# A planner for side work replaced by a fixed table of slots, in an attention block fused with a gated feed-forward

## The chip, the cores and the metric

The kernel runs on one core of one Trainium2 chip. The metric is device microseconds of one execution. A core has five engines with instruction streams of their own, which run in order and wait for each other through semaphores: TensorE (PE, matmuls; PEld is its weight load), VectorE (DVE), ScalarE (ACT), GpSimd (POOL) and SyncE (SP, which here issues DMAs). Lines such as L800 are lines of the kernel before.

## The reference

```python
def _attn_ref(x, inducing):                  # x: 4 x 12416 x 128, inducing: 32 x 128
    ...
    def mab(q, kv):
        s = scale * (q @ kv.transpose(0, 2, 1))
        s = s - s.max(-1, keepdims=True)
        a = np.exp(s)
        a /= a.sum(-1, keepdims=True) + 1e-09
        return a @ kv
    h = mab(I, x)                            # stage 1: 32 queries over 12416 tokens
    return mab(x, h)                         # stage 2: 12416 queries over 32 keys

def _moe_ref(x, w_gate, w_val, w_out):       # 128 -> 1536 -> 128, on all 49664 tokens
    gate = 1.0 / (1.0 + np.exp(-(x @ w_gate)))
    val = x @ w_val
    return gate * val @ w_out
```

The output of the attention block is the input of the feed-forward.

## The kernel before

A batch has 12416 tokens, 97 chunks of 128: six groups of 16 chunks and a group of one chunk (s = 6). Since the second attention has only 32 keys, h is folded into the weights: `hw` holds h times the gate and value weights, and the gate and value of a token are a product of its 32 normalised weights (a2) with `hw`, on 32 rows of TensorE.

**The main loop** (the last lines before the launch) runs over 776 steps, which alternate between a wide one (two of the twelve 128-wide blocks of the hidden layer, tile 128 x 1024) and a narrow one (one block, 128 x 512), for four chunks at a time. A wide and a narrow step are a *slot*: 388 slots, 96 per batch and four at the end for the four one-chunk groups together. In step t, `product(t)` fills v on TensorE (`hidden_mm`, L773), fills the gate of step t + 2, and has VectorE form u = (tanh + 1) * v (L800); `gate(t + 2)` is ScalarE's tanh (L791); `project` adds u times the output weights into `acc` on TensorE (L830), 12 matmuls a slot, and every fourth slot ends in ScalarE's eviction of `acc` (L849) and a store through SP. Gate and value each have one PSUM bank pair and one bank, `acc` has a bank, and one bank, tag `m`, serves all side work.

**A wide product's wait.** It needs tanh(t) and v(t). Where `lag` (what the planner believed ScalarE to be late by) is under LATE, the wait for the tanh is replaced by a wait for the last matmul of the gate fill of t + 2, which itself waits for that tanh.

**Side work** prepares the next batch and the next groups while the loop runs:
- stage 1 of the next batch, per group: `s1_score` (scores in `m` on TensorE, maximum nm on VectorE, L204), `s1_exp` (a1T on ScalarE, L217), `s1_turn_dma` (a1: a transpose by DMA, issued from SP, L241; the one-chunk group is turned on TensorE), `s1_sum` (32 matmuls hp, L253, and the copy hst on ScalarE, L265);
- `combine`: the minimum of minima ml (VectorE, then `join_min` on GpSimd), weights w1 (ScalarE, L355), join hx and its tree (GpSimd, L358 and L297), l_ps and h_ps (L378, L383), li and hT on VectorE, two halves of `hw` (`hw_fill`, copy L394);
- stage 2, per group: `s2_score` (two halves of eight matmuls, L403), `s2_take` (sc on ScalarE, L442), `s2_lower_pool` (maximum tree on GpSimd, L452 to L457), `s2_exp_low` (e on ScalarE, L466), `s2_sum_pool` (L474), `s2_inverse_pool` (L498 ff.) and `s2_spread` (a2n, L520) on GpSimd, `s2_turn_dma` (a2r: a transpose by DMA from SP, L531). The last group of a batch carries the one-chunk group along (17 columns);
- loads: `x_load` (from GpSimd's queue, L92) and `x_transpose_dma` (xT, from SP's queue, L101).

**What sets their order.** Each piece is a Python generator. `beside(slot)`, called after the wide step, and `beside_late()`, called after the narrow one, advance all active generators, stage 2 first, then combine, then stage 1. A generator that says "take" waits for the bank `m`; one that says a number waits until its cost fits a running estimate, `behind`, of how late ScalarE is (it falls by ROOM = 0.33 a slot and rises by EVICT = 0.48 per eviction; large operations go into the late call). Thus the slots in which side work lands differ from group to group. Every engine gets its instructions in the order in which this program issues them.

Of the kernel before, what the change touches and what calls it, by code (L numbers as in the profile page):

```python
# [13 lines left out]
ALU = mybir.AluOpType  # L14
# [8 lines left out]
S1_LAG = 6  # L23
S1_FIRST = 7
S2_LEAD = 28
S2_LAG = 8
COMBINE_LAG = 6
SUM_LAG = 9
ROOM = 0.33
MOST = 0.67  # L30
EVICT = 0.48
SMALL = 0.2
LATE = 0.55
# [3 lines left out]
def kernel(  # L37
# [136 lines left out]
    behind = [0.0]  # L174
# [92 lines left out]
    def stage1(b, s):  # L267
        yield "take"
        s1 = s1_score(b, s, "m")
        behind[0] = max(behind[0] - 0.6, -0.2)  # L270
        yield
        yield 0.48
        a1T = s1_exp(b, s, s1)
        yield "give"
        yield
        if groups[s][1] == GC:
            a1 = s1_turn_dma(b, s, a1T)
            for _ in range(S1_LAG):
                yield
            yield "take"  # L280
        else:
            yield "take"
            a1 = s1_turn_copy(s, s1_turn_pe(b, s, a1T))
            yield
        yield 0.18
        s1_sum(b, s, a1, "m")
        yield "give"
# [55 lines left out]
    def combine(b):  # L343
        q = b % 2
        nm1, hst = nm1s[q], hsts[q]
        while summed[b] < NS:
            yield
        ml = bp.tile([P, 1], F32, tag="ml")
        nc.vector.tensor_reduce(out=ml[:], in_=nm1[:], axis=AX.X, op=ALU.min)
        col = join_min(bp, ml)  # L350
        for _ in range(COMBINE_LAG):
            yield
        yield 0.2
        w1 = bp.tile([P, NS], F32, tag="w1")
        nc.scalar.activation(out=w1[:], in_=nm1[:], func=AF.Exp, bias=col[:], scale=-1.0)  # L355
        yield
        hx = bp.tile([P, NS, C + 1], F32, tag="hx", bufs=1)
        nc.gpsimd.tensor_tensor(  # L358
            out=hx[:],
            in0=hst[:],  # L360
            in1=w1[:].unsqueeze(2).to_broadcast((P, NS, C + 1)),
            op=ALU.mult,
        )
        add_tree(hx, NS)
        e32l = bp.tile([P, m], F32, tag="e32l")
        nc.gpsimd.tensor_scalar(
            out=e32l[:],
            in0=e32[:],
            scalar1=hx[:, 0, C : C + 1],
            scalar2=TINY,  # L370
            op0=ALU.mult,
            op1=ALU.add,
        )
        for _ in range(SUM_LAG):
            yield
        yield "take"
        l_ps = ps.tile([P, m], F32, tag="m", name="l_ps")
        nc.tensor.matmul(l_ps[:], ones[:], e32l[:], start=True, stop=True)  # L378
        li = l_inverse(l_ps[:])
        yield "give"  # L380
        yield "take"
        h_ps = ps.tile([P, m], F32, tag="m", name="h_ps")
        nc.tensor.matmul(h_ps[:], hx[:, 0, 0:C], e32[:], start=True, stop=True)  # L383
        h_take(b, h_ps[:], li)
        yield "give"
        yield


        hwt = bp.tile([P, NI, P], F16, tag="hw", bufs=B)
        for hf in range(2):  # L390
            yield "take"
            hw_ps = hw_fill(b, hf, "m")
            yield 0.37
            nc.scalar.copy(out=hwt[:, ts(hf, NI // 2), :], in_=hw_ps[:])  # L394
            yield "give"
        hw[b] = hwt
# [41 lines left out]

    taking = [0]
# [99 lines left out]
    def stage2(b, c, soon=False, far=0):  # L539
        while b not in hT16 or taking[0]:  # L540
            yield
        taking[0] += not soon
        n = GC + far
        if not soon:
            sc = s2p.tile([P, GC + NLO, m], F32, tag="sc", name="sc", bufs=1)
        if far:
            yield "take"
            s2 = ps.tile([P, GC, m], F32, tag="m", name="s2_ps")
            s2_score(b, 0, 0, far, s2, True)
            yield  # L550
            yield 0.08
            s2_take(sc, GC, far, s2)
            yield "give"
        yield "take"
        s2 = ps.tile([P, GC, m], F32, tag="m", name="s2_ps")
        s2_score(b, c, 0, GC // 2, s2)
        yield
        s2_score(b, c, GC // 2, GC, s2, not soon)
        if soon:
            hi, lo = s2_max(GC, s2)  # L560
            yield
            yield
            yield 0.48
            e = s2_exp(GC, s2, hi, lo)
            yield "give"
        else:
            yield
            yield 0.48
            s2_take(sc, 0, GC, s2)
            s2_lower_pool(n, sc)  # L570
            yield "give"
            for _ in range(S2_LAG):
                yield
            yield 0.48
            e = s2_exp_low(n, sc)
            taking[0] = 0
            yield
        sme = s2_sum_pool(n, e)
        yield
        yield  # L580
        rs = (s2_inverse if soon else s2_inverse_pool)(n, sme)
        a2n = s2_spread(n, e[:, 0:n, :], rs, nc.gpsimd)
        for _ in range(2 if soon else 4 if far else 5):
            yield
        s2_turn_dma(b, c, GC, a2n, "a2r")
        if far:
            s2_turn_dma(b, 0, far, a2n, "a2l", GC)
# [205 lines left out]
    def product(t):  # L793
# [21 lines left out]
    lag = []  # L815
# [4 lines left out]
    def project(upto, now, room):  # L820
        while queue and queue[-1][0] < upto and room > 0:
# [23 lines left out]
            elif j == NJ - 1:  # L845
                behind[0] += EVICT
                block = blocks[st["block"]]
                o32 = op.tile([P, BC, C], F32, tag="o32")
                nc.scalar.mul(out=o32[:], in_=acc[0][0][:], mul=0.5)  # L849
# [6 lines left out]
    work = []  # L856
    loads = []
    base = [first_step[(b, 0)] // 2 for b in range(B)]
    SG = first_step[(0, 1)] // 2
    for b in range(B):  # L860
        at = base[b]
        for s in range(1, NG):
            c = groups[s][0]
            soon = b == 0 and s == 1
            far = NLO if s == NG - 1 else 0
            work.append(
                (
                    max(0, at + SG * s - S2_LEAD),
                    0,
                    lambda b=b, c=c, soon=soon, far=far: stage2(b, c, soon, far),  # L870
                )
            )
        if b + 1 < B:
            for g in range(NS):
                loads.append((at + (5 if b == 0 else 3) * g, "t", b + 1, g))
                if b == 0 and 3 <= g < NG:
                    loads.append((at + (3, 14, 17)[g - 3], "x", 1, g))
                work.append((at + S1_FIRST + 6 * g, 2, lambda b=b, g=g: stage1(b + 1, g)))
            work.append((at + S1_FIRST + 6 * NS, 1, lambda b=b: combine(b + 1)))
            work.append((at + SG * NG - S2_LEAD, 0, lambda b=b: stage2(b + 1, NLO)))  # L880
        if b + 2 < B:
            for g in range(NG):
                loads.append((at + 24 + 9 * g, "x", b + 2, g))
    loads.sort(key=lambda e: e[0])
    work.sort(key=lambda e: e[0])

    active = []
    holder = [None]
    free_at = [0]
    slot_now = [0]  # L890

    def taken():
        return holder[0] is not None or slot_now[0] < free_at[0]

    def fits(cost):
        slot = slot_now[0] % 4
        at = behind[0] + cost
        if cost <= SMALL and slot == 2 and any(g["cost"] > SMALL for g in active):
            return False
        return at <= MOST and at + (EVICT if slot == 0 else EVICT - ROOM if slot == 3 else 0.0) <= MOST  # L900

    def advance(gen, late=False):

        if gen["cost"]:
            if late == (gen["cost"] <= SMALL) or not fits(gen["cost"]):
                return
            behind[0] += gen["cost"]
            gen["cost"] = 0.0
        elif late:
            return  # L910
        if gen["ask"]:
            if taken():
                return
            holder[0] = gen
            gen["ask"] = False
        while True:
            try:
                said = next(gen["it"])
            except StopIteration:
                active.remove(gen)  # L920
                return
            if isinstance(said, float):
# [86 lines left out]
```

## Time and profile before

| | |
|---|---|
| median of 3 runs | 731.3 us (730.89 to 731.36) |
| the profiled execution | 730.88 us, span 729.1 us |
| granted TensorE clock, mean | 0.991 |
| busy, share of the span | DVE 97%, ACT 93%, PE 89%, POOL 57% |
| first product starts, last one ends | 33.3 us, 725.2 us |
| chain that ended last | DVE 53%, issue 23%, PE 14%, ACT 5%, DMA 2% |
| wide product, narrow product | 388 of 1212 ns, 387 of 676 ns |
| wide tanh, narrow tanh | 388 of 1034 ns, 388 of 609 ns |
| a1 transposes, issue to landing | 2.4 / 2.6 / 7.2 us (least, median, most) |
| xT transposes, issue to landing | 2.2 / 4.8 / 11.4 us |

How to read it: durations are those of single instructions in one profiled execution, and neighbours on one engine overlap a little, so sums of durations come out above busy times. A group's line ends with the engine's idle time just before its instructions and what ended it. A wait is put down to the semaphore that came last. In the page, queue q1 carries what SP issues and q0 what GpSimd issues.

### The profile page before, as it was taken

The page shows a single profiled execution, that of the slowest core. Times are in us where ns is not written, and L with a number is a line of the kernel's source. Part 1 is how long each engine was busy: PE and PEld are TensorE (multiplying, and loading weights), DVE is VectorE, ACT ScalarE, POOL GpSimd, SP SyncE. Part 2 cuts the span into 40 slices and gives each one's busy share as a digit, 9 for nine tenths or more (in the row PEclk, how much of TensorE's full clock was granted, in tenths as well). Part 3 has the DMA queues.
Part 4 walks back from the last instruction along what each step waited for, and adds up shares of the span by engine and source line. Part 5 has one row for each costly group of instructions (what it writes and reads, how often), then busy time and mean ns, then how long its engine had stood idle before and what let it go on. Part 6 is the DMA issues. An engine that isn't in the chain of part 4 may idle for free.

```text
span 729.1 us, 21430 instructions
## 1 busy us (share of the span) xinstructions
PE 647.7 (89%) x8406; PEld 393.3 (54%) x8406; DVE 708.5 (97%) x873; ACT 675.6 (93%) x1011; POOL 419.1 (57%) x702
## 2 busy tenths in 40 slices
PE   6798998999998989989988899899999899898887
PEld 4355555555554555555555555555555555555555
DVE  4799999999999999999999999999999999999998
ACT  4689999999999999999999999999999999999996
POOL 3554655886764548488567265388486575555200
PEclk9799999999999999999999999999999999999999
DMA  9899736243259272436148541320222122121211
GB/s 174 142 163 197 154 74 138 60 83 81 75 109 181 51 137 75 95 74 118 45 97 159 110 76 45 74 74 31 75 60 69 49 60 60 51 67 45 60 45 45
DMA packets 117750, 65.19 MB, mean 89 GB/s; under 512 B 101361, under 2 KB 102033, under 8 KB 117649
## 3 DMA queue, kind: packets, MB, share of 16 engines
q1 hardware_dynamic: 111936, 49.81, 29.3%
q0 software_dynamic: 5440, 13.90, 11.2%
q8 instruction: 65, 1.06, 0.6%
q14 instruction: 37, 0.29, 0.1%
q10 hardware_dynamic: 272, 0.13, 0.1%
HBM read 27.80 MB, written 25.43 MB: 73 GB/s over the span
## 4 chain that ended last, share of the span: by engine, by line
DVE 53%; issue 23%; PE 14%; ACT 5%; DMA 2%; POOL 1%; DVEq 1%; ACTq 0%; POOLq 0%
DVE u L800 51%; PE acc_ps L830 6%; PE v_ps L773 5%; ACT t L791 5%; DMA xn<-in_x_dram 2%; DVE nm L204 1%; DVEq L800 1%; PE hp_ps L253 1%; PE g_ps L773 1%; POOL xn L92 0%; PE s_ps L192 0%; ACT a1T L217 0%; POOL sum L474 0%; DVE li L302 0%; PE s_ps L427 0%
## 5 line engine op out<-in xcount | busy, mean ns | idle before, releaser
L800 DVE SCALAR_TENSOR_TENSOR u<-t,v_ps 128x1024 f16<-128x1024 f16 (+1 forms) x777 | 678.1, 943 | 3.0 <-PE g_ps L773 1.3
L791 ACT ACTIVATE t<-g_ps 128x1024 f16<-128x1024 f32 (+1 forms) x776 | 595.1, 822 | 32.8 <-ACT t L791 20.0
L773 PE MATMUL v_ps<-a2r,hwt 32*128 32x512 f16 (+1 forms) x1188 | 293.5, 371 | 65.0 <-DVE u L800 61.8
L830 PE MATMUL acc_ps<-wo,u 128*128 128x128 f16 x4656 | 328.3, 220 | 0.3
L830 PEld LDWEIGHTS <-u 128*128 128x128 f16 x4656 | 262.5, 98 | 89.8 <-issue 88.6
L773 PE MATMUL g_ps<-a2r,hwt 32*128 32x512 f16 (+1 forms) x1188 | 296.6, 377 | 0.0
L773 PEld LDWEIGHTS <-hwt 32*128 32x128 f16 x2400 | 93.3, 91 | 200.6 <-issue 154.8
L474 POOL TENSOR_TENSOR sum<-e 128x256 f32<-128x256 f16 (+1 forms) x23 | 15.4, 670 | 156.1 <-ACT e L466 152.1
L520 POOL TENSOR_TENSOR a2n<-e,rs 128x2048 f16<-128x2048 f16 (+2 forms) x24 | 86.2, 3593 | 6.8 <-PE g_ps L773 2.8
L498 POOL TENSOR_TENSOR near<-sme,minus 128x16 f32<-128x16 f32 (+1 forms) x22 | 65.2, 2965 | 1.7
L849 ACT ACTIVATE o<-acc_ps 128x512 f32<-128x512 f32 x96 | 58.4, 608 | 0.5 <-PE acc_ps L830 0.5
L453 POOL TENSOR_SCALAR rise<-rise 128x256 f32<-128x256 f32 (+6 forms) x110 | 51.0, 463 | 9.7
L452 POOL TENSOR_TENSOR rise<-sc 128x256 f32<-128x256 f32 (+1 forms) x22 | 16.3, 740 | 30.8 <-ACT sc L442 30.8
L454 POOL TENSOR_TENSOR top<-top,rise 128x128 f32<-128x128 f32 (+3 forms) x88 | 28.3, 321 | 7.3
L474 POOL TENSOR_TENSOR sum<-sum 128x128 f32<-128x128 f32 (+3 forms) x92 | 28.3, 308 | 7.2
L452 POOL TENSOR_TENSOR rise<-top 128x128 f32<-128x128 f32 (+3 forms) x88 | 27.2, 309 | 6.9
L457 POOL TENSOR_TENSOR sc<-sc,top 128x512 f32<-128x512 f32 (+1 forms) x22 | 23.9, 1084 | 1.7
L403 PEld LDWEIGHTS <-xT 128*128 128x128 f16 x388 | 13.4, 97 | 12.2 <-issue 12.2
L403 PE MATMUL s_ps<-hT,xT 128*128 128x32 f16 x388 | 18.2, 179 | 0.3 <-DVE hT L307 0.3
L454 POOL TENSOR_TENSOR top<-sc,rise 128x256 f32<-128x256 f32 (+1 forms) x22 | 16.3, 739 | 1.8
L217 ACT ACTIVATE a1T<-s_ps,nm 128x512 f16<-128x512 f32 (+1 forms) x24 | 15.1, 630 | 1.7 <-DVE nm L204 1.7
L204 DVE TENSOR_REDUCE nm<-s_ps 128x1 f32<-128x512 f32 (+1 forms) x24 | 14.7, 614 | 0.9 <-PE s_ps L192 0.9
(116 smaller groups left out, 229.9 us busy)
## 6 DMA issues: line engine op xcount, KB each, us to landing
out_dram<-o SPq DMA_DIRECT2D x96, 256.0 KB, 2.3
xn<-in_x_dram POOLq DMA_DIRECT2D x19, 512.0 KB, 6.8
xn<-in_x_dram POOLq DMA_DIRECT2D x4, 544.0 KB, 5.9
a2r<-a2n SPq DMA_TRANSPOSE x29, 4.6
xn<-in_x_dram POOLq DMA_DIRECT2D x1, 384.0 KB, 15.3
wg<-in_moe_w_gate_dram POOLq DMA_DIRECT2D x1, 384.0 KB, 4.6
wv<-in_moe_w_val_dram POOLq DMA_DIRECT2D x1, 384.0 KB, 6.4
wo<-in_moe_w_out_dram POOLq DMA_DIRECT2D x1, 384.0 KB, 5.2
```

The costliest lines, as they stand in the source:

```text
L403: nc.tensor.matmul(s2[:, j, :], xT[b][:, c + j, :], hT16[b][:], start=(j == 0), stop=whole and j == j1 - 1, skip_group_check=True,)
L452: nc.gpsimd.tensor_tensor(out=r, in0=far, in1=near, op=ALU.subtract)
L453: nc.gpsimd.tensor_scalar_max(out=r, in0=r, scalar1=0.0)
L454: nc.gpsimd.tensor_tensor(out=top[:, 0:n, 0:w], in0=near, in1=r, op=ALU.add)
L474: nc.gpsimd.tensor_tensor(out=d[:, 0:n, :], in0=src[:, :, 0:w], in1=src[:, :, w : 2 * w], op=ALU.add)
L498: nc.gpsimd.tensor_tensor(out=near[:, 0:n], in0=sme[:, 0:n], in1=minus1[:, 0:n], op=ALU.pow)
L520: eng.tensor_tensor(out=a2n[:, 0:n, :, :], in0=e.unsqueeze(2).to_broadcast((P, n, 4, m)), in1=rs.unsqueeze(2).unsqueeze(3).to_broadcast((P ...
L773: st[what + "end"] = nc.tensor.matmul(pt[:, k, col : col + nb * P], hw[b][r : r + 32, j // 2, :], a2r[r : r + 32, o : o + nb, :].rearrange ...
L791: st["tanh"] = nc.scalar.activation(out=st["t"][:], in_=st["g"][:], func=AF.Tanh, scale=0.5)
L800: u = nc.vector.scalar_tensor_tensor(out=st["u"][:, :, c:e], in0=st["t"][:, :, c:e], scalar=1.0, in1=st["v"][:, :, c:e], op0=ALU.add, op1= ...
L830: nc.tensor.matmul(acc[0][(i // 2) % len(acc[0])][:, i, :], st["u"][:, k, ts(i, P)], wo16[:, j, :], start=(j == 0 and i in ((0, 2) if len( ...
L849: nc.scalar.mul(out=o32[:], in_=acc[0][0][:], mul=0.5)
```

## The change

The planner (generators, costs, `behind`, `lag`) is removed. A table `plan` maps a slot and a call (early or late) to a list of closures; `plan_stage1`, `plan_combine` and `plan_stage2` enter the steps of a piece at slots written out by hand, counted from the first slot o of a batch, in a pattern that repeats every 16 slots. The loop then calls what stands at each slot. The functions that issue the instructions stay the same, with these differences: every wide product from step 4 to the last but two waits for the gate fill of t + 2; l and h share one tile of bank `m` and are issued in the same slot; the join of the next h is entered four slots after `least`, two slots before the take and maximum tree of the batch's last group; the one-chunk group is scored before groups 4 and 5; some loads move to other slots.

The core of the diff, with the table in full:

```diff
+    plan = {}
+    def at(slot, make, late=False):
+        plan.setdefault((slot, late), []).append(make)
...
+    def plan_stage1(b, s, score, total):
+        st = {}
+        full = groups[s][1] == GC
+        def begin():
+            st["s1"] = s1_score(b, s, "m")
+        def weigh():
+            st["a1T"] = s1_exp(b, s, st["s1"])
...
+        at(score, begin)
+        at(score + 1, weigh, late=full)
+        at(score + 2, turn)
+        at(total, lambda: s1_sum(b, s, st["a1"], "m"))
...
+    def plan_combine(b, lead, weights, fill):
...
+        def total():
+            lh = ps.tile([P, 2, m], F32, tag="m", name="lh_ps")
+            nc.tensor.matmul(lh[:, 0, :], ones[:], st["e32l"][:], start=True, stop=True)
+            nc.tensor.matmul(lh[:, 1, :], st["hx"][:, 0, 0:C], e32[:], start=True, stop=True)
+            st["lh"], st["li"] = lh, l_inverse(lh[:, 0, :])
...
+        at(lead, least)
+        at(weights, weigh)
+        at(weights + 1, join)
+        at(weights + 8, total)
+        at(weights + 9, lambda: h_take(b, st["lh"][:, 1, :], st["li"]))
+        for hf, (first, second) in enumerate(fill):
+            at(first, lambda hf=hf: part(hf))
+            at(second, lambda hf=hf: keep(hf), late=True)
...
+    def plan_stage2(b, c, score, take, weigh, far=None, soon=False):
...
+        if far is not None:
+            at(far, one)
+            at(far + 1, lambda: s2_take(st["sc"], GC, NLO, st["s2"]))
+        at(score, lambda: half(0, False))
+        at(score + 1, lambda: half(GC // 2, not soon))
         if not soon:
+            at(take, lower, late=True)
+        at(weigh, exp, late=True)
+        at(weigh + 1, total)
+        at(weigh + 3, spread)
+        at(weigh + (5 if soon else 8 if far is None else 7), turn)
...
-        if st["cnt"] == 2 and 4 <= t < NST - 2 and lag[t // 2 - 2] < LATE:
+        if st["cnt"] == 2 and 4 <= t < NST - 2:
...
+        if b == 0:
+            plan_stage2(0, groups[1][0], o, None, o + 3, soon=True)
+            plan_stage2(0, groups[2][0], o + 5, o + 7, o + 18)
+        for s in range(3 if b == 0 else 2, NG - 1):
+            k = o + 16 * s - 28
+            plan_stage2(b, groups[s][0], k, k + 2, k + (14 if more else 10))
+        plan_stage2(b, groups[NG - 1][0], o + 56, o + 58, o + 66, far=o + 52)
+        if not more:
+            continue
+        for s, (score, total) in enumerate(
+            ([(9, 17), (13, 19)] if b == 0 else [(8, 15), (12, 19)])
+            + [(24, 31), (28, 35), (40, 47), (44, 51), (32, 43)]
+        ):
+            plan_stage1(b + 1, s, o + score, o + total)
+        plan_combine(b + 1, o + 52, o + 55, [(o + 72, o + 74), (o + 80, o + 82)])
+        plan_stage2(b + 1, groups[0][0], o + 67, o + 70, o + 78)
+        plan_stage2(b + 1, groups[1][0], o + 84, o + 86, o + 94)
+        for g in range(NS):
+            at(o + (5 if b == 0 else 3) * g, lambda b=b, g=g: x_transpose_dma(b + 1, g))
+            if b == 0 and 3 <= g < NG:
+                at(o + (3, 14, 17)[g - 3], lambda g=g: x_load(1, g))
         if b + 2 < B:
             for g in range(NG):
-                loads.append((at + 24 + 9 * g, "x", b + 2, g))
+                at(o + (24, 33, 42, 60, 60, 82)[g], lambda b=b, g=g: x_load(b + 2, g))
...
+    def beside(slot, late):
+        for make in plan.pop((slot, late), ()):
+            make()
...
         if t % 2 == 0:
-            beside(t // 2)
+            beside(t // 2, False)
         else:
-            beside_late()
+            beside(t // 2, True)
             project(t - 1, t, 3 if waiting(t - 1) <= 3 else 4)
```

In `plan_stage2`, `lower` is the copy sc and the maximum tree, `exp` is e, `turn` the transpose by DMA.

More of the change, by code (lines that the diff above doesn't have):

```diff
@@ L341, in join_min @@
         return top
-    def combine(b):
+    def plan_combine(b, lead, weights, fill):
         q = b % 2
         nm1, hst = nm1s[q], hsts[q]
[L346 to L396, printed above, removed]
@@ new lines, in total, with part, keep @@
+        def total():
[3 more added lines that the diff above has]
+            st["lh"], st["li"] = lh, l_inverse(lh[:, 0, :])
+        def part(hf):
+            st["hw_ps"] = hw_fill(b, hf, "m")
+        def keep(hf):
+            if hf == 0:
+                st["hwt"] = bp.tile([P, NI, P], F16, tag="hw", bufs=B, name="hwt")
+            nc.scalar.copy(out=st["hwt"][:, ts(hf, NI // 2), :], in_=st["hw_ps"][:])
+            if hf == 1:
+                hw[b] = st["hwt"]
@@ L537, in s2_turn_dma @@
             a2[(b, c + j)] = (a2r, j)
[L539 to L543, printed above, removed]
-        if not soon:
[L545 to L587, printed above, removed]
@@ new lines, in plan_stage2, with bank, room, one @@
+    def plan_stage2(b, c, score, take, weigh, far=None, soon=False):
+        st = {}
+        n = GC + (NLO if far is not None else 0)
+        def bank():
+            st["s2"] = ps.tile([P, GC, m], F32, tag="m", name="s2_ps")
+        def room():
+            st["sc"] = s2p.tile([P, GC + NLO, m], F32, tag="sc", name="sc", bufs=1)
+        def one():
+            room()
+            bank()
+            s2_score(b, 0, 0, NLO, st["s2"], True)
+        def half(j0, whole):
+            if j0 == 0:
+                bank()
+            s2_score(b, c, j0, j0 + GC // 2, st["s2"], whole)
+            if soon and j0:
+                st["hl"] = s2_max(GC, st["s2"])
+        def lower():
+            if far is None:
+                room()
+            s2_take(st["sc"], 0, GC, st["s2"])
+            s2_lower_pool(n, st["sc"])
+        def exp():
+            st["e"] = s2_exp(GC, st["s2"], *st["hl"]) if soon else s2_exp_low(n, st["sc"])
+        def total():
+            st["sme"] = s2_sum_pool(n, st["e"])
+        def spread():
+            rs = (s2_inverse if soon else s2_inverse_pool)(n, st["sme"])
+            st["a2n"] = s2_spread(n, st["e"][:, 0:n, :], rs, nc.gpsimd)
+        def turn():
+            s2_turn_dma(b, c, GC, st["a2n"], "a2r")
+            if far is not None:
+                s2_turn_dma(b, 0, NLO, st["a2n"], "a2l", GC)
+        if far is not None:
+            at(far, one)
+            at(far + 1, lambda: s2_take(st["sc"], GC, NLO, st["s2"]))
+        at(score, lambda: half(0, False))
+        at(score + 1, lambda: half(GC // 2, not soon))
+        if not soon:
+            at(take, lower, late=True)
[3 more added lines that the diff above has]
+        at(weigh + (5 if soon else 8 if far is None else 7), turn)
@@ L853, in project @@
                     return
-    work = []
-    loads = []
     base = [first_step[(b, 0)] // 2 for b in range(B)]
-    SG = first_step[(0, 1)] // 2
     for b in range(B):
[L861 to L880, printed above, removed]
+        o = base[b]
@@ L884 @@
[L884 to L900, printed above, removed]
@@ L939, in beside @@
-    def beside(slot):
-        slot_now[0] = slot
-        behind[0] = max(behind[0] - ROOM, 0.0)
-        while loads and loads[0][0] <= slot:
-            _, what, b, g = loads.pop(0)
-            if what == "x":
-                x_load(b, g)
-            else:
-                x_transpose_dma(b, g)
-        while work and work[0][0] <= slot:
-            _, first, make = work.pop(0)
-            active.append(dict(it=make(), ask=False, first=first, cost=0.0))
-        for gen in sorted(active, key=lambda e: e["first"]):
-            advance(gen)
@@ L972 @@
         if t % 2 == 0:
[L973 removed]
+            beside(t // 2, False)
         else:
[L975 removed]
+            beside(t // 2, True)
             project(t - 1, t, 3 if waiting(t - 1) <= 3 else 4)
[L977 removed]
+    assert not plan
     project(NST, NST, 10**6)
```

111 lines of the change are left out of this document (36 added, 75 removed).

## The prediction

> **What bounds the kernel now.** I read the page's busy times first, then the groups kept apart by shape, then who waited for whom, then TensorE's timeline in a quiet and in a crowded stretch, and last the DMAs.
>
> ```profile
> span 729.1 us, 21430 instructions
> ...
> PE 647.7 (89%) x8406; PEld 393.3 (54%) x8406; DVE 708.5 (97%) x873; ACT 675.6 (93%) x1011; POOL 419.1 (57%) x702
> ```
>
> VectorE has 20.6 us of idle time in the whole span, and the first product starts only at 33.3 us, so most of that lies before the main loop. The groups:
>
> ```profile
> L800 DVE SCALAR_TENSOR_TENSOR u<-t,v_ps 128x1024 f16<-128x1024 f16 x388 | 470.2, 1212 | 2.6 <-PE g_ps L773 0.9 <-ACT t L791 0.6
> L791 ACT ACTIVATE t<-g_ps 128x1024 f16<-128x1024 f32 x388 | 401.2, 1034 | 31.8 <-ACT t L791 20.0 <-PE g_ps L773 4.4 <-PE v_ps L773 1.3
> L800 DVE SCALAR_TENSOR_TENSOR u<-t,v_ps 128x512 f16<-128x512 f16 x387 | 261.7, 676 | 0.4 <-PE g_ps L773 0.4
> L849 ACT ACTIVATE o<-acc_ps 128x512 f32<-128x512 f32 x96 | 58.4, 608 | 0.5 <-PE acc_ps L830 0.5
> L466 ACT ACTIVATE e<-sc 128x512 f16<-128x512 f32 x18 | 11.4, 634 | 0.0
> ```
>
> The means overlap by about 80 ns on VectorE: in its timeline a wide product is followed by the next one after 1.131 us and a narrow one after 0.598 us, so a slot (one wide, one narrow) is 1.729 us and 388 slots are 670.9 us. From the first product (33.3) to the end of the last (725.2) are 692.0 us. The difference, 21.1 us, I split by walking L800 from start to start: 13.9 us are VectorE's other instructions (21 maxima, nm, at 0.547 us; the rest li, hT, ml, a, rs, nmx), about 0.3 us is the tail of the last instruction, and 6.9 us are waits. **6.9 us, 0.9%, is all that a better order can win.** VectorE's own work does not change.
>
> The waits, by place: 1.55 us in the first six slots (still filling), 0.41 in the last five, and 4.9 scattered. TensorE shows what makes the scattered ones. A quiet stretch:
>
> ```profile
> 104.49 0.39 PE L773 MATMUL v_ps<-a2r,hwt 32*128 32x512 f16 x2
> ...
> 105.09 0.37 PE L773 MATMUL v_ps<-a2r,hwt 32*128 32x512 f16 x1 [0.20 <-DVE u L800]
> ...
> 105.41 0.84 PE L830 MATMUL acc_ps<-wo,u 128*128 128x128 f16 x12
> 106.22 0.39 PE L773 MATMUL v_ps<-a2r,hwt 32*128 32x512 f16 x2
> ```
>
> and one with a stage-1 sum (hp) between the wide and the narrow fill:
>
> ```profile
> 109.79 0.39 PE L773 MATMUL v_ps<-a2r,hwt 32*128 32x512 f16 x2
> ...
> 110.53 0.38 PE L773 MATMUL v_ps<-a2r,hwt 32*128 32x512 f16 x1
> ...
> 111.63 0.39 PE L773 MATMUL v_ps<-a2r,hwt 32*128 32x512 f16 x2
> ```
>
> Quiet: 1.73 us from wide fill to wide fill, of which TensorE waits 0.20 us for a product before the narrow fill. With hp the narrow fill comes 0.74 us after the wide one instead of 0.60, that wait is gone, and the slot is 1.84 us. So TensorE has some 0.27 us of room per slot for side matmuls and next to none after them: a sum costs about 0.095 us (18 sums, 1.7 us), a half of the folded factors (hw) 0.05 to 0.08 us (6, 0.4 to 0.5 us). What is left, about 2.5 us, is ScalarE's. Start to start its pair of tanh takes 0.920 + 0.476 = 1.396 us, 0.333 us less than a slot; an eviction takes 0.477, a copy sc 0.465, an exponential e 0.519, a1T 0.54, a copy hst 0.146. In a quiet slot the wide tanh ends 0.22 us before the fill that overwrites its bank, so ScalarE may run about 0.19 us late before a product moves. One large operation per slot leaves 0.477 - 0.333 = 0.14 or 0.519 - 0.333 = 0.19 us: free. Two in neighbouring slots, or a large one with hst, are not: e one slot ahead of an eviction cost 0.07 us in each of six places, an eviction next to sc ahead of a sum 0.14 us near 257 us, w1 beside sc 0.12 to 0.38 us in each combine.
>
> **The change, part by part.**
>
> *ScalarE's table (gain).* In the new order evictions stand in every slot = 0 mod 4, e and sc mostly two slots later, a1T one slot after an eviction but behind a maximum that delays VectorE by 0.547 us, hst by itself in an odd slot. Adding up 0.333 us of room per slot against the rows above, lateness at a wide tanh never passes 0.21 us after the first eleven slots. So the crowding goes: by place it is 0.58, 0.75 and 0.64 us in the three batches that prepare a next one, 0.43 us for e beside evictions and 0.06 us in the last: 2.5 us. Two of these waits (0.3 us each) look like single delays of one tanh that may come elsewhere, so 1.9 to 2.5.
>
> *The always-on wait of the wide product for the gate fill.* 34 wide products that waited for their tanh directly now wait for the fill behind it, which adds up to 0.45 us where ScalarE is late; queued behind the product are the narrow one and TensorE's next wide fill. At 0.21 us of lateness it adds 0.02 us; slot 10, where sc and an eviction still stand close, perhaps 0.1. Sum 0.2 us. If the lateness stayed as it was (0.28 to 0.33 us in most of the 34), it would be 0.1 each, 3.4 us.
>
> *Sums and factors on TensorE.* The 18 sums and 6 hw halves stay, one per slot: 0. l_ps and h_ps, each two fp32 passes (0.34 us), now stand in one slot: about 0.65 us against 0.27 of room plus 0.275 us of VectorE's li in that slot, 0.1 us, three times: 0.3 us (0 to 0.4 each).
>
> *The join ahead of the last maximum tree, on GpSimd.* In its timeline of the second batch the sum began at 300.7 us, and with the minimum of minima, inverse and spread it was done at 313.7; join and its tree take 4.4 us, the maximum tree (17 columns) 8.8 us, gaps included: 326.9. The exponential that needs the tree began at 328.3. As the slots between get some 0.4 us shorter, about 1.0 us of cover is left: cost nothing, and each microsecond beyond would stop ScalarE, in three places. The two loads put at slot 60 are queued behind the tree. The next batch's hT comes about five slots earlier, and nothing waits for it.
>
> *DMA issues (loss).* The table fixes when TensorE asks for a transposed tile; before, a sum came six advances after its transpose's issue, and the one-chunk group (s = 6) was scored at slot 45 of the first batch. Now it is scored at slot 32, and its transpose xT is issued at slot 30, behind a1's transpose on SP's queue; TensorE's weight load there waits for it, and behind it everything. On GpSimd the loads of the batch after next, entered at 24 and 33, both stand behind the maximum tree that starts after the spread: e ends at slot 19.1, sum, inverse and spread take 10.2 us, the tree 8.6 us, so both loads go out at about slot 29.2 and 29.6, just ahead of a1 (30.0) and xT (30.7). (Slots are counted from the first product; slot 30 was at 90.4 us, slot 32 at 93.9.) The trace has such meetings. SP's timeline and the DMA issues near 90 us, with microseconds to landing as the last number, no load moving:
>
> ```profile
> 88.97 1.14 SPq L101 DMA_TRANSPOSE xT<-xn  x1
> 90.44 1.20 SPq L241 DMA_TRANSPOSE a<-a1T  x1
> ...
> xT<-xn SPq DMA_TRANSPOSE x1, 2.9
> a<-a1T SPq DMA_TRANSPOSE x1, 2.4
> ```
>
> and beside two loads issued at 118.81 us (packets by queue in 121.2 to 124.2 us, then the a1 issue at 118.69):
>
> ```profile
> q0 software_dynamic: 159, 0.59, 98.7%
> q1 hardware_dynamic: 48, 0.01, 2.6%
> ...
> a<-a1T SPq DMA_TRANSPOSE x1, 7.2
> ```
>
> While the loads (q0) move, SP's queue gets 48 small packets through in 3 us, and the a1 transpose lands 7.2 us after its issue instead of 2.4. Beside the pair at 59.4 us a larger xT took 11.4 us. Counted from the first load, 7.1 us is slot 33.3 and the small xT comes behind a1: about 33.8. TensorE is there at 32.05: 1.75 slots, **3.0 us**, once. The ends: 0.6 us (xT alone, 2.9 us, lands at 32.4) and 6 us (as beside 59.4). I take 3.0, as a1 is the size of the row with 7.2.
>
> [...]
>
> The other meetings have cover: a1 of slot 30 in the second batch would land near 33.5 and is wanted at 35; a1 of slot 46 meets one load and is wanted at 51; a2r of slot 86 is wanted at 95.
>
> **Sum.** -2.5 (crowding) + 0.2 (gate fill) + 0.3 (l and h) = -2.0; +3.0 for xT: +1.0 us. The profiled execution took 730.88 us (span 729.1 and 1.8 around it), 0.4 below the median; I add the difference to the median: 732.3. About 0.2% (1.46 us) is what a measurement of this kernel can tell from no change, so this counts as the same.
>
> **Rivals.**
> 1. *The transpose is in time.* The loads go out earlier or later than I work out, or share fairly. Cost 0 to 0.6 us, sum -2.0 to -1.4: 729.5. For it: a1 at 90.44 us, with a load 1.2 us behind it, landed in 2.4 us. Against: both loads are queued directly behind the tree. Chance 0.20, 0.18 of it beyond 0.2%.
> 2. *Slower: xT waits for the second load's end too.* The second of the pair landed 7.9 us after its issue, which is slot 34.1; transposes behind a pair ended up to 0.7 slots after it. Landing at 34.7 costs 4.5 us: +2.5, 733.8. It decides from a landing at slot 34.1 on (3.5 us). Chance 0.20.
> 3. *The gain does not come*: the scattered waits are TensorE's as much as ScalarE's, or the new fill waits eat it. For it: nearly all name g_ps as releaser. Then -0.3 + 3.0: 734.0. Chance 0.11.
> 4. *GpSimd's chain overruns* its 1.0 us of cover by 0.5 us, three times, on top of the sum: 733.8. Chance 0.07.
>
> That the change doesn't do what it says I exclude: the order of ScalarE's instructions is the table's.
>
> **Numbers.** Likeliest, 0.42: 732.3, by itself 731.6 to 732.7. Faster 0.18; same 0.42 + 0.02 = 0.44; slower 0.20 + 0.11 + 0.07 = 0.38. The range runs from the first rival's lower end, 729.2, to 734.0.
>
> **What would show it.** Right: waits of products of 0.06 us and more survive only behind sums, hw and lh; one wait of TensorE for xT near 94 us of some 3 us, with two loads issued 4 to 5 us before it. Wrong: no such wait (rival 1); ScalarE waiting for GpSimd at e (rival 4); products waiting after sums for a1; or the crowding unchanged in size.

## Result, and the profile after

The changed kernel took 733.7 us (median of 8 executions, 732.62 to 735.06) against 731.18 us for the kernel before on the same chip: the ratio is 1.0032, 95% interval 1.0021 to 1.0044, so it is slower by about 2.5 us. The forecast was 732.3 us, in a range of 729.2 to 734.0. The profiled execution of the changed kernel, 735.06 us, is the longest of its eight.

```profile
span 733.3 us, 21425 instructions
...
PE 646.6 (88%) x8406; PEld 392.1 (53%) x8406; DVE 707.0 (96%) x873; ACT 676.3 (92%) x1011; POOL 419.1 (57%) x702
```

VectorE works 1.5 us less than before (708.5) and the span is 4.2 us longer, so its idle time has grown from 20.6 to 26.3 us. The groups of the profile, kept apart by shape (busy time, mean of one, and after the bar the idle time ahead of them):

```profile
L802 DVE SCALAR_TENSOR_TENSOR u<-t,v_ps 128x1024 f16<-128x1024 f16 x388 | 469.0, 1209 | 5.0 <-PE g_ps L775 4.0 <-PE aT_ps L223 0.5
...
L802 DVE SCALAR_TENSOR_TENSOR u<-t,v_ps 128x512 f16<-128x512 f16 x387 | 260.7, 674 | 0.7 <-PE g_ps L775 0.7
L849 ACT ACTIVATE o<-acc_ps 128x512 f32<-128x512 f32 x96 | 57.9, 604 | 0.8 <-PE acc_ps L831 0.8
```

L802 is L800 of before, L775 and L831 are L773 and L830. The products' busy time is the same to 0.4%. The idle time ahead of the wide products went from 2.6 to 5.0 us, and none of it is put down to ScalarE's tanh any more (0.6 us before). The list of waits says where the largest of it is (who waits for whom: sum, times, longest):

```profile
PEld L185 <- DMA xT<-xn: 5.2, 1, 5.2
PE s_ps L185 <- DMA xT<-xn: 4.9, 1, 4.9
DVE nm L197 <- PE s_ps L185: 4.9, 2, 4.0
```

One wait of TensorE for one transposed tile, 4.9 us. It is the one of the forecast: GpSimd sends the two loads out at 89.88 us, SP issues the a transpose and then the xT transpose, and both are long in flight (timelines of GpSimd and SP; then the queues' packets from 91.2 to 97 us, and the time from issue to landing):

```profile
89.88 1.19 POOL L81 DMA_DIRECT2D xn<-in_x_dram  x2
```
```profile
91.20 1.57 SPq L234 DMA_TRANSPOSE a<-a1T  x1
92.82 1.24 SPq L90 DMA_TRANSPOSE xT<-xn  x1
```
```profile
q0 software_dynamic: 260, 1.03, 99.6%
q1 hardware_dynamic: 75, 0.02, 2.5%
...
a<-a1T SPq DMA_TRANSPOSE x1, 8.1
xT<-xn SPq DMA_TRANSPOSE x1, 6.7
```

The loads' queue (q0) moves 260 packets and SP's (q1) 75 in these 5.8 us. The a transpose lands at 99.3 us and xT at 99.5 us; TensorE had been ready at 94.7. What the forecast did not have is the clock. In the table by stretches the first number after the engines is the granted TensorE clock:

```profile
96.00:98.00 2.00, 0.00 (x0) 0.00 (x0) 0.00 (x0) 0.00 (x0) 0.00 (x0) 1.00 1.45 193
98.00:100.00 2.00, 0.43 (x3) 0.20 (x3) 0.11 (x1) 0.00 (x0) 0.00 (x0) 0.73 0.28 14
100.00:102.00 2.00, 2.00 (x18) 1.33 (x18) 0.86 (x2) 0.77 (x2) 0.00 (x0) 0.50 0.01 4
102.00:104.00 2.00, 2.00 (x18) 1.20 (x12) 1.62 (x2) 1.99 (x4) 0.00 (x0) 0.50 0.34 130
104.00:106.00 2.00, 2.00 (x21) 1.20 (x19) 1.46 (x4) 1.37 (x3) 0.00 (x0) 0.56 0.01 1
106.00:110.00 4.00, 4.00 (x84) 2.50 (x81) 3.98 (x6) 3.92 (x8) 2.59 (x7) 1.00 0.01 4
```

From 60 to 98 us the clock was 1.00. From 98.9 us, near the end of the idle stretch, it is halved for 6.8 us (to 105.8 in finer slices), and TensorE, busy all of that time, falls behind VectorE, whose busy time in the row of 100 to 102 us is 0.86 of 2.00 us.

A sum (hp) in a slot looks as it did before: TensorE's timeline has 0.74 us from the wide to the narrow fill and 1.84 us from wide to wide.

```profile
92.42 0.39 PE L775 MATMUL v_ps<-a2r,hwt 32*128 32x512 f16 x2
...
93.16 0.38 PE L775 MATMUL v_ps<-a2r,hwt 32*128 32x512 f16 x1
...
94.26 0.39 PE L775 MATMUL v_ps<-a2r,hwt 32*128 32x512 f16 x2
```

Walking the products from start to start, as the prediction did, splits the 4.2 us between the two profiled executions: first product 0.94 us earlier; the first six slots (the filling stage) 2.03 us more waiting; xT 6.33 us (4.41 at nm behind the one-chunk score, 1.92 in the two slots after it); scattered waits 5.3 us before, 2.2 after, 3.1 less (those of the last five slots counted in). The sum is +4.3. So two large terms of opposite sign, and one, the filling stage, that the text below puts down to chance.

### The profile page after: what moved, and what is told of

It is laid out like the page before. It is cut to its first block, busy times and chain, and to the rows that moved or that the text cites. A ratio compares the mean times of both kernels' runs of the same rounds, so it can differ in the third digit from the quotient of the medians.

```text
span 733.3 us, 21425 instructions
## 1 busy us (share of the span) xinstructions
PE 646.6 (88%) x8406; PEld 392.1 (53%) x8406; DVE 707.0 (96%) x873; ACT 676.3 (92%) x1011; POOL 419.1 (57%) x702
## 4 chain that ended last, share of the span: by engine, by line
DVE 56%; issue 24%; PE 8%; ACT 6%; DMA 3%; POOL 1%; DVEq 1%; ACTq 0%; POOLq 0%; SPq 0%
DVE u L802 53%; ACT t L793 6%; PE acc_ps L831 4%; PE v_ps L775 3%; DMA xn<-in_x_dram 2%; DVE nm L197 2%; DMA xT<-xn 1%; DVEq L802 1%; PE g_ps L775 0%; POOL xn L81 0%; POOL sum L471 0%; PE s_ps L402 0%; PE s_ps L426 0%; PE hp_ps L246 0%; DVE li L294 0%
## 5 line engine op out<-in xcount | busy, mean ns | idle before, releaser
L802 DVE SCALAR_TENSOR_TENSOR u<-t,v_ps 128x1024 f16<-128x1024 f16 (+1 forms) x777 | 676.3, 940 | 5.7 <-PE g_ps L775 4.7
L775 PE MATMUL v_ps<-a2r,hwt 32*128 32x512 f16 (+1 forms) x1188 | 294.6, 373 | 66.9 <-DVE u L802 65.1
L831 PE MATMUL acc_ps<-wo,u 128*128 128x128 f16 x4656 | 331.2, 221 | 0.0
L831 PEld LDWEIGHTS <-u 128*128 128x128 f16 x4656 | 264.4, 98 | 90.6 <-issue 89.8
L775 PE MATMUL g_ps<-a2r,hwt 32*128 32x512 f16 (+1 forms) x1188 | 298.0, 380 | 0.0
L775 PEld LDWEIGHTS <-hwt 32*128 32x128 f16 x2400 | 90.2, 91 | 201.4 <-issue 157.7
L197 DVE TENSOR_REDUCE nm<-s_ps 128x1 f32<-128x512 f32 (+1 forms) x24 | 14.6, 610 | 4.9 <-PE s_ps L185 4.9
```

Of the source, the lines that this page charges most:

```text
L775: st[what + "end"] = nc.tensor.matmul(pt[:, k, col : col + nb * P], hw[b][r : r + 32, j // 2, :], a2r[r : r + 32, o : o + nb, :].rearrange ...
L802: u = nc.vector.scalar_tensor_tensor(out=st["u"][:, :, c:e], in0=st["t"][:, :, c:e], scalar=1.0, in1=st["v"][:, :, c:e], op0=ALU.add, op1= ...
L831: nc.tensor.matmul(acc[0][(i // 2) % len(acc[0])][:, i, :], st["u"][:, k, ts(i, P)], wo16[:, j, :], start=(j == 0 and i in ((0, 2) if len( ...
```

## The experiments: the lost microseconds

The kernel before ran beside each group of runs; its medians were 731.07 (e1 to e4), 731.81 (e5 to e8) and 731.00 us (e9, e10). Each group ran on a chip of its own, so a difference between medians of two groups is uncertain by some 0.8 us.

**e1: the transpose earlier.**

```diff
-            at(o + (5 if b == 0 else 3) * g, lambda b=b, g=g: x_transpose_dma(b + 1, g))
+            at(o + ((5 * g if g < NG else 22) if b == 0 else 3 * g), lambda b=b, g=g: x_transpose_dma(b + 1, g))
```

> The changed kernel with one number different: the first batch's one-chunk xT transpose is entered at slot 22 instead of slot 30, ahead of the pair of x loads. Theory (the whole loss is this one transpose: 4.4 us of waiting at nm plus 1.9 us of the half clock after it): no wait of TensorE for xT near 95 to 100 us, granted clock 1.0 there, 733.7 - 6.3 = 727.4 us, which is 0.5% faster than the kernel before. Rival (the loss is the filling stage, whose first six slots waited 2.0 us longer, and the wait for xT is made up later): the wait goes but the time stays at 732 to 733.5 us.

Measured: 727.64 us, ratio to before 0.9957 (0.9943 to 0.9970). The theory holds: 6.1 us between the medians, against 6.3. xT was issued at 73.9 us, with no load moving, and landed long before it was needed:

```profile
xT<-xn SPq DMA_TRANSPOSE x1, 2.2
```

No wait for xT is left, the clock stays at 1.00 from 40 us on, and the wide products have

```profile
L802 DVE SCALAR_TENSOR_TENSOR u<-t,v_ps 128x1024 f16<-128x1024 f16 x388 | 471.4, 1215 | 1.4 <-PE g_ps L775 1.0
```

1.4 us of idle time ahead of them, where the changed kernel had 5.0 and the kernel before 2.6. With one number changed, the table is 3.4 us faster than the kernel before. The first six slots of this run waited 1.5 us, as before, with the very instructions of the changed kernel.

**e2: the loads later.**

```diff
-                at(o + (24, 33, 42, 60, 60, 82)[g], lambda b=b, g=g: x_load(b + 2, g))
+                at(o + ((36, 36) if b == 0 else (24, 33))[g] if g < 2 else o + (42, 60, 60, 82)[g - 2],
+                   lambda b=b, g=g: x_load(b + 2, g))
```

> The changed kernel with the two x loads of the third batch that were entered at slots 24 and 33 entered at slot 36; the xT transpose stays at slot 30 behind a1. Theory (the loads' packets starve the transpose): xT lands within about 3 us of its issue, TensorE waits at most 0.6 us for it, the clock stays at 1.0, 727.4 to 728.5 us. Rival (the transpose is simply issued too late, behind a1 on SP's queue): the wait of 4 to 5 us and the half clock stay, 733 to 734 us. Third possibility: the loads only starve another transpose from slot 36 on; then a new wait shows in its place.

Measured: 730.05 us, ratio 0.9983 (0.9975 to 0.9992). Both causes are real: of the 6.1 us, 3.65 go with the loads and 2.4 stay. The flights, with no load moving:

```profile
a<-a1T SPq DMA_TRANSPOSE x1, 2.4
xT<-xn SPq DMA_TRANSPOSE x1, 3.9
```

Here xT took 3.9 us, not the 2.9 that I had used, and TensorE waited 1.7 us. The expected bound of 0.6 us was wrong. The a transpose, issued 1.2 us ahead of xT on the same queue, is the nearest reason; this is not shown, for in e1 xT landed in 2.2 us although a 512 KB transpose, issued 4.2 us ahead of it, was still in flight on that queue.

**e7: the order on SP's queue turned round.**

```diff
-            at(o + (5 if b == 0 else 3) * g, lambda b=b, g=g: x_transpose_dma(b + 1, g))
+            at(o + (5 * g if b == 0 else 3 * g) - (b == 0 and g == NG),
+               lambda b=b, g=g: x_transpose_dma(b + 1, g), late=b == 0 and g == NG)
```

> The changed kernel with the order on SP's queue turned round at slot 30: the one-chunk xT transpose is issued late in slot 29, ahead of the a transpose and not behind it, but still in the same microsecond as the pair of loads. Theory (both the loads and the place behind a count: with the loads away, run e2, 2.4 of 6.1 us stayed): xT no longer waits for a's packets but still meets the loads, lands some 5 to 7 us after its issue, about 96 to 97.5 us; wait 0.5 to 2.5 us, 728.5 to 731 us. Rival (only the loads count): landing near 98 us as before, 733 us. Other rival (only the place behind a counts): lands in about 3 us, no wait, 727.6 us.

Measured: 729.49 us, ratio 0.9968 (0.9956 to 0.9979), within the theory's range. xT was issued at 89.69 us, 3.1 us sooner, flew 6.5 us beside the loads, and TensorE waited 1.7 us. So the loads lengthen the flight (6.5 to 6.7 us with them, 3.9 without), and the place behind a delays the issue; either alone leaves 1.7 us of waiting, both together 4.9.

This run also shows a halved clock after only 1.7 us of idle time (TensorE's timeline, then the table by stretches):

```profile
96.22 0.23 PE L185 MATMUL s_ps<-xT,indT 128*32 128x128 f16 x1 [1.70 <-DMA xT<-xn]
```
```profile
98.00:100.00 2.00, 1.85 (x19) 1.50 (x19) 1.74 (x2) 1.80 (x4) 0.00 (x0) 0.56 0.56 166
100.00:102.00 2.00, 2.00 (x23) 1.27 (x16) 1.74 (x3) 1.68 (x3) 0.00 (x0) 0.59 0.00 0
```

In finer slices it lasts from 98.2 to 101.6 us, 3.4 us, half of the 6.8 us in the changed kernel.

**e3: TensorE kept busy while xT is in flight.**

```diff
+        for _ in range(20 if (b, s) == (1, NG) else 0):   # ahead of the one-chunk score
+            nc.tensor.matmul(s1[0:32, :], indT[:],
+                xT[b][:, NLO : NLO + 4, :].rearrange("c j t -> c (j t)"), start=True, stop=True)
```

> The changed kernel with 20 extra 512-column matmuls on TensorE (about 4.3 us of them, results overwritten) just ahead of the one-chunk score at slot 32, so that TensorE works while xT is in flight. Nothing else is changed. Theory (the half clock after the wait comes from TensorE's idle time): the wait of VectorE at nm stays at 4 to 5 us, the granted clock stays at 1.0 in the 10 us behind it, and the 1.9 us of waits at the two slots behind go: 733.7 - 1.9 = 731.8 us. Rival (the clock drop has another cause, such as the burst of work that follows): the clock drops all the same, 733.5 to 734.5 us.

Measured: 732.42 us, ratio 1.0018 (1.0009 to 1.0027): 1.3 us below the changed kernel, 4.8 above e1. The wait stayed, the clock did not fall:

```profile
98.00:100.00 2.00, 1.31 (x7) 0.48 (x5) 0.00 (x0) 0.00 (x0) 0.00 (x0) 1.00 0.88 36
```
```profile
DVE nm L206 <- PE s_ps L194: 5.0, 2, 4.1
```

The theory holds in its mechanism: the clock was 1.00 in all of the 12 us from 98 us on. In size it brought 1.3 us for 1.9. In the trace 0.45 of the 1.92 us stayed at the first wide product after the score, so this part is the refilling of the gate and not the clock's; the clock's own price is 1.47 us by the trace and 1.3 by the medians.

In these traces the clock does not go with the length of the idle stretch alone. In the changed kernel it fell at 98.9 us, within the 4.9 us without work (94.7 to 99.6), and was low for 6.8 us; in e7 it fell at 98.2 us, 2.0 us after 1.7 us without work had ended, and was low for 3.4 us; e2 had the same 1.7 us and in its profiled execution kept 1.00. What decides between them, no run shows.

**e10: e2 with TensorE kept busy.** The same lines as e3, 8 matmuls, in e2.

> Run e2 (loads away from the xT transpose, 730.05 us) with 8 extra 512-column matmuls on TensorE, about 1.7 us, results overwritten, ahead of the one-chunk score at slot 32: they fill the 1.7 us in which TensorE waits for xT. Theory (in most executions of e2, though not in the profiled one, the 1.7 us of idle time is followed by a stretch at half clock as in e7, worth about 1.2 us): 728.8 us, as the profiled execution of e2. Rival (the clock has no part in e2's remaining loss): 730 us.

Measured: 729.29 us, ratio 0.9977 (0.9968 to 0.9986), whose interval overlaps that of e2. Seven of its 11 executions lie between 728.7 and 729.4 us, of e2's 11 only one. This points the theory's way, that many executions of e2 paid for a halved clock that its profile does not show; it is not shown, since only the profiled execution has a clock by place. The filling stage is a rival for the spread: its waits alone differ from 1.5 to 3.8 us between the profiled executions of this text.

## The experiments: the gained microseconds

**e4: the always-on wait alone, in the old order.**

```diff
-        if st["cnt"] == 2 and 4 <= t < NST - 2 and lag[t // 2 - 2] < LATE:
+        if st["cnt"] == 2 and 4 <= t < NST - 2:
```

> The kernel before with one line of the change alone: every wide product of the main loop waits for the gate fill two slots on, not only those where ScalarE was planned to be little late. ScalarE's crowded order stays. My bound, 0.1 us at each of 34 products: 731.2 + 3.4 = 734.6 us. Rival (a product that is late has its fill done just as late anyway, about 0.02 us each): 731.2 to 731.9 us, no difference. Neither theory of the changed kernel's loss needs this part; it prices it.

Measured: 731.37 us, ratio 1.0004 (0.9995 to 1.0013): no difference; the bound of 3.4 us was far too high. The trace shows two parts that cancel. In the kernel before, 29 wide products have a semaphore instruction of VectorE's own right ahead of them, and 2.3 us of the waits lie there; in e4 there are 5, with 0.07 us. The waits ahead of the other wide products rose from 3.7 to 6.4 us, so the wait for the fill does cost 2.7 us in the old order, near the bound; what I had left out is the 2.2 us that it saves.

**e5: e1 without that wait anywhere.**

```diff
-        if st["cnt"] == 2 and 4 <= t < NST - 2:
+        if st["cnt"] == 2 and t < 0:
```

> Run e1 (one-chunk xT at slot 22, 727.6 us) with the manual wait of the wide products for the gate fill taken out altogether: every product waits for its own tanh, as the scheduler puts it. It prices the always-on wait in the fixed table. Theory (ScalarE is never more than 0.21 us late there, so the wait is worth about 0.2 us in all): 727.4 us, no difference that can be told. Rival (the wait is what removed the small waits): 1 us or more slower. Other rival (the wait costs 0.1 us at each of the 34 products that had none before): up to 3 us faster, 724.5 us.

Measured: 742.22 us, ratio 1.0139 (1.0124 to 1.0155): 14.6 us slower than e1 (14.7 between the spans of the two profiled executions). The first rival has the sign, and I had the size wrong by ten times. Without the wait a wide product depends on ScalarE (its tanh) and on TensorE (its v), and 328 of the 388 wide products get a semaphore instruction between the product before and themselves. Such a product starts 34 ns late (median), and the narrow one behind it 7 ns: the walk from start to start gives 14.2 us at those 328 and 2.6 at the narrow ones, 18.3 us of waits in all where e1 has 3.7. Of the 14.2 us, 10.2 are 296 delays of 20 to 50 ns, and some 4 are longer waits at 18 places. That the semaphore instruction is what costs the 34 ns is read from where the delays stand and not isolated: of the 59 wide products without one, 21 start on time, but 28 start some 21 ns late, so part of it may be the direct wait for ScalarE. With the wait for the gate fill, which TensorE does after tanh anyway, one wait of one engine covers everything (5 wide products of e1 have a semaphore instruction ahead of them, where e5 has 328), and the semaphore instructions stand ahead of the narrow product, in the shadow of the 1.13 us of the wide one.

**e8: ScalarE's crowding put back.**

```diff
-            plan_stage2(b, groups[s][0], k, k + 2, k + (14 if more else 10))
+            plan_stage2(b, groups[s][0], k, k + 2, k + (12 if more else 10))   # on e1
```

> Run e1 with the exponential e of eight stage-2 groups put two slots earlier, into the slot of an eviction: ScalarE has two large operations in one slot there, as in the old order. Theory (ScalarE's room of 0.333 us per slot decides: 0.477 + 0.519 - 0.333 = 0.66 us late, 0.19 to 0.22 of it free): a wait of 0.44 to 0.47 us at each of the eight, 3.5 to 3.8 us in all, 731.2 us. Rival (the scattered waits were TensorE's and the table on ScalarE brought nothing): no difference, 727.6 us.

Measured: 734.68 us, ratio 1.0042 (1.0029 to 1.0054), 7.0 us above e1 and not 3.6. At the eight places the ledger is right: five waits of 0.49 us and three of 0.38 (0.30, and 0.08 two slots on), 3.6 us. The rest is a second mechanism, at slot 56 of each of the three batches, 0.94 us each:

```profile
ACT w L348 <- POOL top L332: 3.0, 3, 1.1
```

The exponential two slots earlier puts spread ahead of the minimum of minima on GpSimd (spread 133.8 to 137.4 us, top not before 139.2); in e1 the minimum of minima comes first (131.1 to 133.7). So w waits for GpSimd, and tanh stands behind w. These two make 6.4 of the 7.0 us; the rest is about the 0.7 us by which the kernel before was slower beside e8 than beside e1. This is also the price of an order on GpSimd that does not fit the table; in the table as given ScalarE never waits for GpSimd in the main loop.

**e6 and e9: the sums in two halves.** On e1, the 32 matmuls of a sum are put into two neighbouring slots; e9 moves four of the places.

```diff
-            ([(9, 17), (13, 19)] if b == 0 else [(8, 15), (12, 19)])
-            + [(24, 31), (28, 35), (40, 47), (44, 51), (32, 43)]
+            ([(9, (16, 17)), (13, 19)] if b == 0 else [(8, (15, 16)), (12, (18, 19))])                 # e6
+            + [(24, (30, 31)), (28, 35), (40, (46, 47) if b else (47, 48)), (44, (50, 51)), (32, 43)]
+            ([(9, (16, 17)), (13, 23)] if b == 0 else [(8, (14, 15)), (12, (18, 19))])                 # e9
+            + [(24, 31), (28, 35), (40, (46, 47)), (44, (50, 51)), (32, 43)]
```

> Run e1 with the stage-1 sums (hp) of five of the seven groups of each batch cut into two halves in neighbouring slots (four of them in the first batch): the same matmuls, 16 and 16 instead of 32 in one slot. Theory (what is left of the scattered waits is TensorE's 0.27 us of room per slot overrun by a whole sum, 0.098 us each at 14 places): those 14 waits go, -1.3 us, 726.3 us. Rival (the half that comes earlier waits for the a transpose, or each half still overruns): no gain or a new wait of TensorE for a, 727.5 us or more.

> Run e6 with its sums moved off the slots in which a cut one still waited: halves at 14 and 15 instead of 15 and 16 (second and third batch), at 46 and 47 in all batches, the group at slot 31 whole again, and the first batch's second sum at slot 23 instead of 19, where its a transpose landed too late. Theory (a half waits only where it shares a slot with an eviction or the late a): left of the scattered waits are three of 0.1 us at slot 31 and the last five slots, about 1.6 us less than in e1: 726.0 us. Rival (the scattered waits only move, as from e1 to e6): 727.5 us, no difference from e1.

Measured: e6 727.50 us, ratio 0.9941 (0.9928 to 0.9953); e9 727.17, ratio 0.9946 (0.9933 to 0.9958). Both are faster than the kernel before, neither can be told from e1. The waits at a cut sum do go at most places, but a half waits 0.14 us where it shares its slot with other side work, and in e9 the sum at slot 23 waited 0.41 us for its bank, which ScalarE's copy sc had not yet freed. The scattered waits fell by some 0.5 us in e6 instead of 1.3; the rival, that they move, is nearer. e1, e6 and e9 all beat both kernels.

## Why the prediction was right, and which terms were off

The forecast of 732.3 us missed the median by 1.4 us. That is partly luck, for two larger errors cancel: the wait for xT cost 3.1 us more than forecast and the gain was 1.4 us more. By the forecast's own line of 0.2%, 2.5 us is slower, which had a chance of 0.38, and not the same, which had 0.44.

**What bounds the kernel** was right: of the 6.9 us of waits that were given as all there is to win, e1 won 3.4 us, and e9 and e6 won 3.8 and 4.3 us against the kernel before beside them.

**The transposed tile** was the right wait at the right place, with the right causes: the loads went out at slots 29.3 and 29.6 (29.2 and 29.6 forecast), a at 30.0, and TensorE waited at slot 32. The size, 3.0 us, is the step that failed: it measured 6.1 us by the medians, 6.3 in the trace, above the 6 us that the text gave as the upper end. Three things are in the difference of 3.3 us in the trace. xT landed some 1.8 us later than at slot 33.8, of which VectorE felt 1.4 (4.4 us at nm). The gate had to be refilled, 0.45 us. And the halved clock cost 1.3 to 1.5 us, which nothing in the text allowed for.

Behind the late landing stands the row of 7.2 us. It was right by size and wrong by its place: its transpose was issued at 118.69 us, 0.1 us ahead of its pair of loads, and the text counted 7.1 us from the first load. Here a was issued 1.3 us behind the first load and landed 9.4 us after it (8.1 from its own issue). The traces of all runs with the new table have 26 a transposes that were issued 0.6 to 2.9 us behind the second load of a pair, and each landed 0.4 to 0.6 us after that load. The two that the kernel before issues ahead of a pair (118.69 and 290.44 us) landed some 1.5 us before the second load did. Why the order of issue decides this, no run shows.

**The gain** was 3.4 us, not 2.0. In the ledger of e1 the waits outside the first and the last slots are 1.9 us, of 4.9 before; the forecast left 2.9. Of the 1.0 us between, 0.5 are the two losses that did not come: l_ps and h_ps in one slot cost nothing (the three li took 0.80 us of VectorE's time from start to start, 0.82 before), and the always-on wait is no loss. Some 0.4 us came from the sums and hw: 15 sums wait, 14 of them 0.098 us each, not 18, and the hw halves less. Outside the waits, the first product of e1 started 0.2 us earlier. Waits of 0.06 us and more are left in e1 behind those 15 sums and one half of hw, as forecast, and at two other places, 0.08 us each. That ScalarE's crowding costs what was worked out, e8 shows by putting it back. But part of what I booked as crowding, 24 products that waited 32 ns or more with a semaphore instruction ahead of them, was in part the form of the wait, some 34 ns each, 0.8 us, if that price holds there; my 0.2 us of loss for the always-on wait had the wrong sign.

**Rivals.** 1, the transpose in time, is what e1 makes true by hand, at 727.6 us and not 729.5, as the gain was larger. 2, xT waits for the second load's end, is what happened: the second load, 8.3 us in flight, landed at 98.9 us, a at 99.3 and xT at 99.5 (below, the two loads, with the time from issue to landing as the last number). The likeliest case had xT land some 1.8 us ahead of that. Its 4.5 us was the better price for the wait itself (4.4 at nm), and its 733.8 us is the median to 0.1, but by errors that cancel: the wait cost 1.8 us more by the trace (1.6 by the medians) and the gain was 1.4 us more. 3, the gain does not come, falls with e1. 4, GpSimd's chain, did not happen; e8 shows what a wait of ScalarE for GpSimd costs at another place, 0.94 us each.

```profile
xn<-in_x_dram POOLq DMA_DIRECT2D x1, 544.0 KB, 5.6
xn<-in_x_dram POOLq DMA_DIRECT2D x1, 512.0 KB, 8.3
```

**The filling stage** was forecast as unchanged. In the two profiled executions it was 2.0 us longer after the change, because the half clock at the start lasted until 44.3 us instead of 39.6. All runs but e4 and e5 have the instructions of the changed kernel up to slot 9, and in their profiled executions it ended between 39.1 and 40.8 us in four (e1, e2, e9, e10), at 41.9 in e6 and between 43.6 and 45.2 in three (e3, e7, e8): it goes with the execution and not with the change. In the walks of all twelve traces the waits of the first six slots rise with this end without exception, from 1.5 us (39.1) to 3.8 (45.2). Why it ends where it does was not tried.

## What to carry to other kernels

When side work is moved to fixed places, check for each DMA not only its order in its queue but what else is in flight at the moment of issue and how long the engine that needs it will stand still. Take the flight from a row in which the transfers were issued in the same order: here one 32 KB transpose, eight slots too late, ate more than a whole reordering won (6.1 us against 3.4). A wait that looks like an extra dependency can be cheaper than the one it replaces, if it turns two waits for two engines into one, as here by 14.6 us (e5 against e1); count the waits of the instruction on the critical engine before pricing it. And price an idle stretch of TensorE with the half clock that may come behind it (1.3 us here, the changed kernel against e3).

## What the runs showed of the hardware that was not expected

- A single idle stretch of TensorE of 4.9 us came with 6.8 us at a granted clock of 0.50, one of 1.7 us with 3.4 us in the profiled e7 and with none in the profiled e2. With TensorE kept busy in place of the 4.9 us (e3) there was none.
- A wide product with a semaphore instruction directly ahead of it started 34 ns late (median of 328 in e5; the delays of 20 to 50 ns add up to 10.2 us). Behind a wide product of 1.13 us, ahead of the narrow one, it cost nothing (e1, median of 352).
- A 32 KB transpose from SBUF to SBUF took 2.2 us with no load moving (e1), 3.9 issued 1.2 us behind a 128 KB transpose (e2), and 6.5 to 7.0 beside two loads of 544 and 512 KB (e7, the changed kernel, e3). In the changed kernel the loads' queue moved 260 packets from 91.2 to 97 us, while the transposes' queue moved 75; what sets this proportion, no run shows.
